# A layernorm, MLP and memory-attention kernel with its gradients: chains issued in a hand-written order, 512-wide output projections, left-over rows inside the forward chain

## Chip, cores and metric

The kernel runs on one core of one Trainium2 chip. The metric is the device time of one execution in microseconds. The engines are TensorE (PE, with its weight loads as PEld), VectorE (DVE), ScalarE (ACT), GpSimd (POOL) and SyncE (SP, which here issues the DMAs). SBUF is the on-chip memory, PSUM the memory that PE writes its results to.

## The reference

The output is the input plus two branches on its layernorm: an MLP with a squared ReLU, and an attention that runs over segments of 32 rows with 8 rows of memory. The kernel computes the output and the ten gradients of `jax.vjp`.

```python
xn = layernorm(x)                                   # (2048, 512)
out = x + A(xn, mem0, Wq, Wk, Wv, Wo) + (relu(xn @ w1 + b1) ** 2) @ w2 + b2

def A(x, mem, Wq, Wk, Wv, Wo):                      # 32 heads of 128
    for s in range(64):
        h = concat([mem, x[32 * s:32 * s + 32]])    # 8 + 32 = 40 rows
        q, k, v = h @ Wq, h @ Wk, h @ Wv
        p = softmax(where(mask, q @ k.T * 128 ** -0.5, -1e9))
        o = (p @ v) @ Wo                            # sum over heads
        mem, out_s = o[:8], o[8:]                   # 32 output rows
    return concat(outs)
```

The memory that a segment starts with is made by the segment before. So the 64 segments run one after the other, forward, and again backward for the gradients.

## The kernel before

**Rows.** A segment has 40 rows: 8 of memory, 32 of input. The kernel packs them so that 4 groups of heads (HG) times 32 rows fill the 128 partitions, with 8 heads (KH) side by side in each group. 32 of the 40 rows, the memory and the last 24 input rows, make the *chain*. The first 8 input rows of a segment, the *left-over rows*, do not enter the next memory as queries, so their projections can be done ahead and their attention later, for four segments at once: 16 blocks of 4 × 8 = 32 rows. Their keys and values still take part in the chain's attention.

**Stages, in order of time.** (1) Layernorm, the MLP and its gradients, weight transposes; the change doesn't touch these. (2) Left-row projections: 16 blocks, three tensors each (lines 558 to 571). (3) The forward chain: 64 segments (585 to 656). (4) The left-over loop: 16 blocks, forward and backward of the left-over rows (673 to 736). (5) The backward chain: 64 segments from last to first (807 to 925). (6) A tail, in which `slot_side` gathers the operands of the weight gradients from DRAM, and (7) the weight gradients (956 and 970), 16 groups of 160 matmuls.

**One forward segment.** `proj` (401) multiplies the transposed rows hT (512 × 32, in four pieces of 128) with the resident weights Wqkv: the four head groups go to four strips of 32 partitions. `flip` (181) transposes the result per head with PE, through a PSUM tile. `scores` (425, with the mask at 419), `softmax` (435 to 439), `norm` (445 to 450), `turn` (458) and `weigh` (469, scaled at 474) make the weighted values ON; these are flipped into OT, and `gather` multiplies OT with Wo (484). Heads come in three parts, PARTS = ((0, 3), (3, 3), (6, 2)), so projections are 384, 384 and 256 columns wide. `gather` here sums over all 32 heads in place:

```python
for k in ks:
    for g in range(HG):
        for c in range(DC):     # four strips: the four 128-column pieces of the output
            nc.tensor.matmul(R[32 * c:32 * c + 32, 0:P], lhsT=XT[:, k, g, :], rhs=W[:, g * KH + k, c * P:(c + 1) * P], ...)
```

That is 128 matmuls of 128 columns for 8 × 4 heads. R then holds the 32 output rows; ACT casts it (Rb, 623), PE transposes it (ps_m), and ACT copies the first 8 rows into the next hT (632), to which POOL has copied the 24 input rows. `rest`, played during the next segment, flips the values, and writes what the backward chain needs to DRAM: R as float32 (S_RF) and as bf16 (S_MBF), queries, keys and values (S_NA), probabilities (S_PA) and so on.

**One left-over block.** All DMA reads go into the pool `ls`, which has one buffer of each tile that is used late (l_N, l_kvM), and `ld`, which has two. `fetch_rows` (531, 532) reads the chain's rows and the left rows back from S_RF, to add them to the MLP branch and write the output.

**One backward segment.** The gradient rows goT are projected with WoT (401) and flipped (181), multiplied with the values (425), turned into gradients of the scores on DVE (494 to 500), and `outer` (508) makes the gradients of values, keys and queries: 192 matmuls of 16 to 40 columns. Three gathers (484) multiply these with the three transposed weights WT[2], WT[1], WT[0] into R (ps_gR). bRb (890), a transpose ps_bm and a copy (899) carry 8 rows to the segment before. `rest` flips all three gradients back (`spill_nat`, 24 transposes) and stores them to S_G. Every fourth segment also plays `left_done` (the left-over rows' gathers, ps_gRL, and their spill) and `finish_back` (layernorm's backward and the store).

**What sets the order.** The code is written segment by segment, and a scheduler orders the instructions of each engine by its own costs and priorities; the engines run their queues in order. All DMAs of these stages are issued by SP's queue. The tile pools decide which buffer a tile gets, and a tile whose buffer is still read waits.

Of the kernel before, what the change touches and what calls it, by code (L numbers as in the profile page):

```python
# [12 lines left out]
P = 128  # L13
# [13 lines left out]
def kernel(  # L27
# [80 lines left out]
    assert SEG == 32 and SPB == 4 and H == 32 and NL == 32 and 2 * KK == KH and KK * P == 512  # L108
    AROWS = NSEG * SEG
    NROW = AROWS + NB * NL  # L110
    RC_ALL = NROW // P

    PARTS = ((0, 3), (3, 3), (6, 2))
# [14 lines left out]
    S_TM = dram.tile([NB, P, 2, KH, HG, NL], BF16, name="S_TM")  # L128
    S_VTA = dram.tile([NSEG, P, KH, HG, L], BF16, name="S_VTA")
    S_PA = dram.tile([NSEG, P, KH, L], BF16, name="S_PA")  # L130
    S_PG = dram.tile([NB, P, 2, KH, 2 * NL], BF16, name="S_PG")
# [4 lines left out]
    S_RF = dram.tile([NSL, DC, SEG, P], F32, name="S_RF")  # L136
    S_RB = dram.tile([NSL, DC, SEG, P], F32, name="S_RB")
# [36 lines left out]
    zeros_bf = const.tile([M, D], BF16, name="zeros_bf")  # L174
    nc.vector.memset(zeros_bf[:], 0.0)
# [198 lines left out]

    def sb(name, bufs, side=None):
        return tc.tile_pool(name=name, bufs=bufs, side=side, reuse_waits="tile")
# [4 lines left out]
    def act_copy(out, in_):  # L381
        nc.scalar.copy(out, in_)  # L382

    def dve_copy(out, in_):
        nc.vector.tensor_copy(out, in_)  # L385
# [4 lines left out]
    def make_ops(big, trp, scp, wk, sm):  # L390
        def pbig(name):
            return big.tile([P, 512], F32, name=name, tag="big")

        def proj(dst, hT, W, col0, part, copy):

            k0, nk = part
            ps = pbig("ps_proj")
            for dc in range(DC):
                for g in range(HG):
                    c = col0 + g * GW + k0 * P  # L400
                    nc.tensor.matmul(ps[32 * g:32 * g + 32, 0:nk * P], lhsT=hT[:, dc, :], rhs=W[:, dc, c:c + nk * P],  # L401
                                     start=(dc == 0), stop=(dc == DC - 1), tile_position=(0, 32 * g))
            copy(dst[:, k0 * P:(k0 + nk) * P], ps[:, 0:nk * P])

        def flip(dst, srcN, part, copy):

            k0, nk = part
            ps = trp.tile([P, 1024], BF16, name="ps_tr", tag="tr")
            for k in range(nk):
                transpose_to(ps[:, k * P:(k + 1) * P], srcN[:, (k0 + k) * P:(k0 + k + 1) * P])  # L410
            copy(dst, ps[:, 0:nk * P].rearrange("p (k g r) -> p k g r", k=nk, g=HG))

        def scores(qT, kTs, part, mask):

            k0, nk = part
            sc = scp.tile([P, 512], F32, name="ps_sc", tag="sc")
            sc3 = sc[:, 0:nk * KW].rearrange("p (k n) -> p k n", k=nk)
            if mask is not None:
                nc.tensor.matmul(sc3, lhsT=ident[:], rhs=mask[:, 0:nk, :], start=True, stop=False,
                                 skip_group_check=True)  # L420
            for k in range(nk):
                c = 0
                for kT, n in kTs:
                    for g in range(HG):
                        nc.tensor.matmul(sc3[32 * g:32 * g + 32, k, c:c + n], lhsT=qT[:, k0 + k, g, :],
                                         rhs=kT[:, k0 + k, g, :], start=(mask is None), stop=True,
                                         tile_position=(0, 32 * g), skip_group_check=True)
                    c += n
# [581 lines left out]
```

## Time and profile before

| | us |
|---|---|
| median of 3 runs | 5021.1 |
| lowest and highest run | 5014.1, 5024.96 |
| the profiled execution | 5070.06 |
| its span, first to last instruction | 5068.2 |
| PE busy in the span | 3680.1 |
| weight loads (PEld) busy | 2250.3 |
| DVE, ACT, POOL busy | 1507.3, 1253.2, 313.2 |

The span has 89788 matmuls and 89874 weight loads, and a mean granted PE clock of 0.844. The profile's views give a line of the code for each group of instructions, the tile that it writes and, behind "<-", what it reads; numbers behind a name are buffers. "PEclk" is the share of the full clock that PE was granted. A row of a waits view says: engine, tile, line <- what ended the wait: us in total, times, longest. "issue" is time in which the engine waited for nothing that the profile shows. Windows count from the span's start.

### The profile page before, as it was taken

The page shows a single profiled execution, that of the slowest core. Times are in us where ns is not written, and L with a number is a line of the kernel's source. Part 1 is how long each engine was busy: PE and PEld are TensorE (multiplying, and loading weights), DVE is VectorE, ACT ScalarE, POOL GpSimd, SP SyncE. Part 2 cuts the span into 40 slices and gives each one's busy share as a digit, 9 for nine tenths or more (in the row PEclk, how much of TensorE's full clock was granted, in tenths as well). Part 3 has the DMA queues.
Part 4 walks back from the last instruction along what each step waited for, and adds up shares of the span by engine and source line. Part 5 has one row for each costly group of instructions (what it writes and reads, how often), then busy time and mean ns, then how long its engine had stood idle before and what let it go on. Part 6 is the DMA issues. An engine that isn't in the chain of part 4 may idle for free.

```text
span 5068.2 us, 195611 instructions
## 1 busy us (share of the span) xinstructions
PE 3680.1 (73%) x89788; PEld 2250.3 (44%) x89874; DVE 1507.3 (30%) x5110; ACT 1253.2 (25%) x3450; POOL 313.2 (6%) x741
## 2 busy tenths in 40 slices
PE   3950658878888888844446888787888788659999
PEld 1520223444444444422224666566666566524444
DVE  5530002333333333323333333333333333300000
ACT  1310014333333333311111222222222222201111
POOL 0000000111111111100000000000000000000000
PEclk8975989898888988866666888888888888879999
DMA  4377564233333233355443333333333333388886
GB/s 144 115 172 215 163 235 173 95 102 104 109 106 105 99 105 104 105 213 155 151 146 129 110 113 106 108 113 110 113 105 106 116 110 112 111 160 174 175 174 133
DMA packets 459571, 670.79 MB, mean 132 GB/s; under 512 B 172129, under 2 KB 285434, under 8 KB 456442
## 3 DMA queue, kind: packets, MB, share of 16 engines
q1 hardware_dynamic: 458746, 658.28, 43.9%
q8 instruction: 702, 11.50, 1.0%
q14 instruction: 123, 1.01, 0.1%
HBM read 347.75 MB, written 289.94 MB: 126 GB/s over the span
## 4 chain that ended last, share of the span: by engine, by line
PE 59%; DMA 14%; issue 8%; DVE 8%; ACT 8%; SPq 3%; POOL 0%; ACTq 0%; POOLq 0%; DVEq 0%
PE ps_proj L401 11%; PE ps_gR L484 11%; PE ps_gw L956 7%; PE ps_tr L181 5%; PE ps_R L484 4%; PE ps_nat L181 3%; PE ps_gkq L508 3%; PE ps_gwo L970 3%; DMA l_kvM<-S_NA 2%; PE ps_gRL L484 2%; PE ps_wgh L469 2%; DVE ON L474 2%; ACT OT L382 2%; DMA S_WT<-wtt 1%; DMA ghn<-S_GH1N 1%
## 5 line engine op out<-in xcount | busy, mean ns | idle before, releaser
L401 PE MATMUL ps_proj<-Wqkv,hT 128*32 128x384 bf16 x9216 | 569.0, 349 | 0.6 <-ACT hT L581 0.3
L956 PEld LDWEIGHTS <-HNc 128*128 128x128 bf16 x1920 | 187.5, 98 | 316.3 <-issue 93.9
L484 PE MATMUL ps_gR<-WT_39551,gk 128*32 128x128 bf16 x8192 | 238.9, 274 | 69.2 <-issue 55.3
L401 PEld LDWEIGHTS <-hT 128*32 128x32 bf16 x9216 | 223.1, 103 | 127.7 <-issue 36.9
L469 PEld LDWEIGHTS <-ET 32*32 32x32 bf16 (+1 forms) x5120 | 113.3, 104 | 315.1 <-issue 296.3
L382 ACT CAST gk<-ps_gkq 128x192 bf16<-128x192 f32 (+1 forms) x256 | 70.0, 274 | 717.5 <-PE ps_gkq L508 717.5
L484 PE MATMUL ps_gR<-WT_48383,gq 128*32 128x128 bf16 x8192 | 204.4, 265 | 33.4 <-issue 32.1
L484 PE MATMUL ps_gR<-WT_39549,gv 128*32 128x128 bf16 x8192 | 205.3, 255 | 29.0 <-issue 27.9
L385 DVE CAST gk<-ps_gkq 128x192 bf16<-128x192 f32 (+1 forms) x256 | 73.4, 287 | 512.8 <-PE ps_gkq L508 512.7
L484 PE MATMUL ps_R<-Wo,OT 128*32 128x128 bf16 x8192 | 170.7, 238 | 75.8 <-ACT OT L382 75.4
L484 PEld LDWEIGHTS <-gk 128*32 128x32 bf16 x8192 | 176.6, 122 | 101.6 <-issue 67.3
L401 PE MATMUL ps_proj<-WoT,goT 128*32 128x384 bf16 (+1 forms) x3072 | 207.0, 320 | 19.0 <-POOL goT L798 18.6
L474 DVE TENSOR_TENSOR ON<-ps_wgh,sm_rs 128x384 bf16<-128x384 f32 (+1 forms) x192 | 97.9, 510 | 404.5 <-PE ps_wgh L469 404.5
L484 PEld LDWEIGHTS <-gq 128*32 128x32 bf16 x8192 | 178.4, 123 | 45.7 <-issue 44.9
L385 DVE COPY gNat<-ps_nat 128x512 bf16<-128x512 bf16 x240 | 101.9, 424 | 308.9 <-PE ps_nat L181 308.9
L484 PEld LDWEIGHTS <-gv 128*32 128x32 bf16 x8192 | 164.0, 115 | 44.4 <-issue 37.5
L484 PEld LDWEIGHTS <-OT 128*32 128x32 bf16 x8192 | 133.0, 105 | 111.7 <-ACT OT L382 111.7
L469 PE MATMUL ps_wgh<-l_kvM,ET 32*32 32x128 bf16 x512 | 41.2, 299 | 192.3 <-DMA l_kvM<-S_NA 190.3
L382 ACT COPY gNat<-ps_nat 128x512 bf16<-128x512 bf16 x240 | 140.7, 586 | 144.0 <-PE ps_nat L181 140.9
L508 PEld LDWEIGHTS <-b_QK 32*128 32x128 bf16 x4096 | 123.3, 93 | 93.6 <-issue 68.0
L347 PE MATMUL ps_w_2827<-ghn,xnN 128*128 128x512 bf16 x16 | 6.5, 405 | 191.0 <-DMA ghn<-S_GH1N 191.0
L382 ACT COPY OT<-ps_tr 128x384 bf16<-128x384 bf16 (+1 forms) x192 | 85.2, 444 | 212.2 <-PE ps_tr L181 208.2
(952 smaller groups left out, 6957.4 us busy)
## 6 DMA issues: line engine op xcount, KB each, us to landing
S_G<-gNat SPq DMA_DIRECT2D x80, 768.0 KB
b_QK<-S_NA SPq DMA_DIRECT2D x64, 512.0 KB
S_VTA<-vT SPq DMA_DIRECT2D x64, 320.0 KB
b_vT<-S_VTA SPq DMA_DIRECT2D x64, 320.0 KB
S_O<-ON SPq DMA_DIRECT2D x64, 256.0 KB
ghn<-S_GH1N SPq DMA_DIRECT2D x32, 448.0 KB
an<-S_AN SPq DMA_DIRECT2D x32, 448.0 KB
S_WT<-wtt SPq DMA_DIRECT2D x48, 256.0 KB
```

The lines of the kernel that those rows point to most:

```text
L181: nc.tensor.transpose(ps_ap, in_ap, ident[base:base + k, base:base + k])
L347: nc.tensor.matmul(pss[k][:, :nf], lhsT=xnN[:, rc, dc * P:(dc + 1) * P], rhs=ghn[:, f0g:f0g + nf], start=(rc == 0), stop=(rc == TC - 1),)
L382: nc.scalar.copy(out, in_)
L385: nc.vector.tensor_copy(out, in_)
L401: nc.tensor.matmul(ps[32 * g:32 * g + 32, 0:nk * P], lhsT=hT[:, dc, :], rhs=W[:, dc, c:c + nk * P], start=(dc == 0), stop=(dc == DC - 1), ...
L469: nc.tensor.matmul(ps[32 * g:32 * g + 32, k * P:(k + 1) * P], lhsT=ET[32 * g:32 * g + n, k, i, :], rhs=V[32 * g:32 * g + n, (k0 + k) * P:( ...
L474: nc.vector.tensor_tensor(out=dst[:, k0 * P:(k0 + nk) * P].rearrange("p (k e) -> p k e", k=nk), in0=ps[:, 0:nk * P].rearrange("p (k e) -> ...
L484: nc.tensor.matmul(R[32 * c:32 * c + 32, 0:P], lhsT=XT[:, k, g, :], rhs=W[:, g * KH + k, c * P:(c + 1) * P], start=(first and k == ks[0] a ...
L508: nc.tensor.matmul(out(ps[g], k), lhsT=N_[32 * g:32 * g + m, k * P:(k + 1) * P], rhs=X(k)[32 * g:32 * g + m], start=first, stop=last, tile ...
L956: nc.tensor.matmul(ps[:], lhsT=HNc[:, rc, dc * P:(dc + 1) * P], rhs=gn[:, rc, u * 512:(u + 1) * 512], start=(rc == 0), stop=(rc == RC_ALL ...
L970: nc.tensor.matmul(ps[:], lhsT=on[:, rc, i * P:(i + 1) * P], rhs=GOc[:, rc, :], start=(rc == 0), stop=(rc == RC_ALL - 1))
```

## The change

**Order.** The forward chain, the left-over rows' backward and the backward chain run under `tc.manual_schedule()`: every instruction stands in the order in which Python plays it. Each step of a segment is a small function with a name (`k0mm` projects the first half of the keys, `k0fl` flips it, `k0Te` copies it out of PSUM, and so on), and one table for each chain lists the names in order: F_ORDER, LB_ORDER and B_ORDER. Slots in the tables (F0 to F2, X0 to X2, and others) take left-over work from F_FILL and B_FILL.

**Halves.** Heads go in two halves of 4, so every projection is 512 columns wide: 32 matmuls a tensor, where the three parts took 48.

**Gather.** `gather` now puts the four *head groups* into the four strips and streams all 512 output columns: 32 matmuls of 512 columns. The four strips then hold four partial sums, which are copied to SBUF as float32 (`ra` on ACT, `rv` on DVE, 256 columns each) and added by `sumup`, four matmuls with the float32 selection matrix `sel`. These leave the result transposed, as the next segment needs it, so Rb, ps_m and hT's copies go.

**On chip.** The transposed rows of all segments stay in SBUF: HT (forward) and GT (backward), each 512 × 2048, into whose segment slices the 8 memory rows are cast. S_MBF, S_MBB, S_RF and S_RB go. XT collects the rows of a block, and `block_rows` transposes them on PE.

**Left-over rows.** Their forward is played inside the forward chain, one block during the four segments behind it (the last block alone, after the chain). Their backward is a loop of its own, `lback`, with two buffers and a prefetch of one block. WT is loaded after its first block.

**PSUM.** `ring` makes one tile of one or two banks with two slots a bank for flips (f_tr, b_tr) and scores (f_sc, b_sc); the backward outer products use halves of one four-bank tile (b_pp). Most other tiles of the chains have one buffer.

**Tail.** `slot_side` loads S_HT and S_GM whole and transposes them on PE, 64 transposes each; GOc is made after the first group of products.

In PE's program, the end of a forward segment; before, OT is the operand of the gather, Rb the cast result, N the next tile to flip:

```order
L484 LDWEIGHTS OT
L484 MATMUL ps_R<-Wo,OT 32x128
L181 LDWEIGHTS Rb
L181 MATMUL ps_m<-ident,Rb 128x128
L181 LDWEIGHTS N_15540
L181 MATMUL ps_tr<-ident,N_15540 128x128
```

After, at the same place (f_N holds the segment's projections, f_sc is the ring of the scores):

```order
L457 LDWEIGHTS f_OT
L457 MATMUL ps_R<-Wo,f_OT 32x512
L464 MATMUL f_sc<-sel,R_7758 128x32 x4
L184 LDWEIGHTS f_N
L184 MATMUL f_tr<-ident,f_N 128x128
```

The cast and the transpose of R gave way to four matmuls of 32 columns, and the flip of the values that `rest` held now follows directly.

In DVE's program, the border between two backward segments, before:

```order
L385 CAST gk<-ps_gkq 128x2x32
L385 CAST gq<-ps_gkq 128x2x32
L385 CAST gkL<-ps_gkq 128x2x8
L901 COPY bRf<-ps_gR 128x128
L385 COPY gNat<-ps_nat 128x512 x6
L385 COPY gOT<-ps_tr 128x384 x2
L494 TENSOR_TENSOR ds_t<-ps_sc,b_P 128x120
L496 TENSOR_REDUCE ds_r<-ds_t 128x3
L498 TENSOR_TENSOR ds_u<-ps_sc,ds_r 128x120
```

After (R_50154 is the float32 copy of the gather, GT the gradient rows, gNat a gradient flipped back):

```order
L390 COPY R_50154<-ps_gR 128x256
L390 CAST GT<-b_sc 128x4x8
L390 COPY gNat<-b_tr 128x512 x2
L390 COPY b_XT<-b_sc 128x4x24
L390 COPY gNat<-b_tr 128x512 x2
L390 CAST gON<-ps_proj 128x512
L481 TENSOR_TENSOR ds_t<-b_sc,b_P 128x160
L485 TENSOR_REDUCE ds_r<-ds_t 128x4
L489 TENSOR_TENSOR ds_u<-b_sc,ds_r 128x160
```

DVE now carries the memory rows itself, between half of the copy of R and the copies of the flipped gradients, and one of the two casts of the projection.

In SP's program, the DMAs of one left-over block, before:

```order
L682 DMA l_kvM<-S_NA 32x1x2048 x4
L679 DMA l_TM<-S_TM 128x2048
L531 DMA l_acc<-S_RF 24x4x128 x4
L734 DMA bb<-S_B 128x512
L701 DMA S_O<-l_ON 128x1024
L704 DMA S_RF<-l_Rf 128x128
L685 DMA l_gT<-S_GT 128x4x128
L717 DMA S_GOL<-l_gON 128x1024
L532 DMA l_acc<-S_RF 8x4x128 x4
L677 DMA l_T<-S_TL 128x3072
L718 DMA S_PG<-l_PG 128x1024
L729 DMA S_GQL<-gqL 128x1024
```

After, one round of `lback`:

```order
L883 DMA l_gT<-S_GT 128x4x128
L884 DMA l_vTM<-S_VTM 128x1024
L885 DMA l_vTL<-S_TL 128x1024
L886 DMA l_P<-S_PL 128x512
L888 DMA l_kM<-S_NA 32x1x1024 x4
L889 DMA l_kL<-S_NL 128x1024
L931 DMA S_GOL<-l_gON 128x1024
L932 DMA S_GSL<-l_gS 128x512
L933 DMA S_GQL<-l_gq 128x1024
```

The reads of the next block now stand ahead of this round's stores, which are those of the block before; the output's reads and stores have moved into the forward chain.

The diff, cut to its core:

```diff
-    PARTS = ((0, 3), (3, 3), (6, 2))
-    S_MBF = dram.tile([NSEG, DC, SEG, P], BF16, name="S_MBF")
-    S_MBB = dram.tile([NSEG, DC, SEG, P], BF16, name="S_MBB")
+    S_HT = dram.tile([P, DC, S], BF16, name="S_HT")
+    S_GM = dram.tile([P, DC, S], BF16, name="S_GM")
...
+    sel = const.tile([P, SEG], F32, name="sel")
+    nc.vector.tensor_reduce(sel[:], identF[:].rearrange("p (g r) -> p r g", g=HG), axis=AX.X, op=ALU.add)
...
-        def gather(R, XT, W, ks, first, last):
-            for k in ks:
+    def gather(R, XT, W, h, first, last):
+        for k in range(4 * h, 4 * h + 4):
+            for g in range(HG):
+                nc.tensor.matmul(R[32 * g:32 * g + 32, :], lhsT=XT[:, k, g, :], rhs=W[:, g * KH + k, :],
+                                 start=(first and k == 4 * h), stop=(last and k == 4 * h + 3),
+                                 tile_position=(0, 32 * g))
+    def sumup(sc, R4):
+        for c in range(DC):
+            nc.tensor.matmul(sc[:, c * SEG:(c + 1) * SEG], lhsT=R4[:, c * P:(c + 1) * P], rhs=sel[:],
+                             start=True, stop=True)
+    def ring(pool, banks, width, dt, name):
+        t = pool.tile([P, 2 * banks, width], dt, name=name)
+        n = [0]
+        def take(_):
+            n[0] += 1
+            return t[:, n[0] % (2 * banks)]
+        return take
...
+    F_ORDER = (
+        "ld kl k0mm k1mm k0ev k1ev q0mm q0ev q1mm k0fl k1fl q1ev k0Te q0fl k1Te q0Te v0mm q1fl v0ev q1Te s0 s1 km "
...
+    with sb("fw", 1) as fw, psum("fbig", 4) as fbig, psum("fps", 1) as fps, ExitStack() as fstack:
+        HT = fw.tile([P, DC, S], BF16, name="HT")
+        dma(HT[:], S_XNT[:])
+        tr = ring(fps, 2, 4 * P, BF16, "f_tr")
+        scp = ring(fps, 2, 4 * KW, F32, "f_sc")
...
+            o["rv"] = lambda: vcp(st["R4"][:, 256:512], ps["R"][:, 256:512])
+            def HTf():
+                if s + 1 < NSEG:
+                    vcp(HT[:, :, (s + 1) * SEG:(s + 1) * SEG + M], crows(ps["S"])[:, :, 0:M])
...
+        with tc.manual_schedule():
+            for s in range(NSEG):
+                tables.append(fwd(s))
+                b, j = divmod(s, SPB)
+                if j == 0 and b > 0:
+                    lefts[b - 1] = left(b - 1)
+                play(F_ORDER, tables, s, F_LAG)
...
+            for b in range(NB + 1):
+                play(LB_ORDER, [x[0] for x in lb], b, LB_LAG)
+                if b == 0:
+                    for t in (2, 1, 0):
+                        dma(WT[t][:], S_WT[:, t, :, :])
...
+    with sb("bq", 1) as bq, sb("bs", 2) as bs, sb("bt", 1) as bt, psum("bpp", 1) as bpp, psum("bbig", 2) as bbig, \
+            psum("bps", 1) as bps:
+        GT = bq.tile([P, DC, S], BF16, name="GT")
+        pp = bpp.tile([P, 4, 512], F32, name="b_pp")
+        tr = ring(bps, 1, 4 * P, BF16, "b_tr")
+        scp = ring(bps, 1, 4 * KW, F32, "b_sc")
...
+            sT = p5.tile([P, DC, S], BF16, name="sT", tag="sT")
+            dma(sT[:], srcT[:])
+            for rc in range(TC):
+                ps = p5tr.tile([P, 4 * P], BF16, name="ps_side", tag="tr")
+                for dc in range(DC):
+                    transpose_to(ps[:, dc * P:(dc + 1) * P], sT[:, dc, rc * P:(rc + 1) * P])
```

More of the change, by code (lines that the diff above doesn't have):

```diff
@@ L534, with play @@
+    ENG = {"A": acp, "V": vcp}
+    def play(order, tables, s, lag):
+        for nm in order:
+            t = s - (1 if nm in lag else 0)
+            if 0 <= t < len(tables) and nm in tables[t]:
+                tables[t][nm]()
     wo_cm = sb("wo", 1, "right")
```

1092 lines of the change are left out of this document (626 added, 466 removed), and 10 rows, old and new, of tables (B_FILL, F_FILL).

## The prediction

> **What bounds the kernel now.** I read the slices of the page first, then the table of busy time by stage. Of the page, the granted clock in the 40 slices and the queue of instruction pages:
>
> ```profile
> PEclk8975989898888988866666888888888888879999
> q8 instruction: 702, 11.50, 1.0%
> ```
>
> The stages are left-row projections, forward chain, left-over loop, backward chain, tail, weight grads (columns: us; busy time of PE, PEld, DVE, ACT, POOL with instructions; PEclk; DMA share; GB/s):
>
> ```profile
> 705.00:882.00 177.00, 135.87 (x1928) 62.86 (x1932) 38.36 (x69) 69.96 (x124) 5.71 (x19) 0.91 0.57 208
> 882.00:2187.00 1305.00, 1055.23 (x25738) 590.47 (x25730) 489.66 (x1722) 466.99 (x1276) 181.90 (x505) 0.88 0.30 102
> 2187.00:2722.00 535.00, 215.52 (x7063) 138.67 (x7059) 169.34 (x425) 80.22 (x180) 43.28 (x68) 0.62 0.53 173
> 2722.00:4403.00 1681.00, 1359.77 (x50259) 1031.80 (x50260) 621.27 (x2566) 455.64 (x1593) 70.82 (x109) 0.85 0.34 107
> 4403.00:4486.00 83.00, 8.88 (x365) 7.24 (x366) 4.62 (x11) 3.24 (x7) 3.57 (x3) 0.59 0.86 181
> 4486.00:5068.00 582.00, 554.01 (x2508) 249.56 (x2557) 0.00 (x0) 75.02 (x128) 0.00 (x0) 1.00 0.78 164
> ```
>
> The two chains are 64 segments each: 1305/64 = 20.4 us and 1681/64 = 26.3 us a segment, with PE busy 81% of both. The left-over loop has PE busy 40% and 535/16 = 33 us a block. What ends PE's waits, in the left-over loop, in the forward chain, in the backward chain:
>
> ```profile
> PE ps_wgh L469 <- DMA l_kvM<-S_NA: 190.3, 60, 9.7
> PE ps_sc L425 <- DMA l_acc<-S_RF: 42.3, 1, 42.3
> ```
> ```profile
> PE ps_R L484 <- ACT OT L382: 75.2, 176, 0.6
> PE ps_tr L181 <- DVE ON L474: 75.2, 128, 0.7
> ```
> ```profile
> PE ps_gR L484 <- issue: 112.8, 132, 2.4
> PE ps_gkq L508 <- issue: 76.9, 59, 2.6
> PE ps_gRL L484 <- issue: 49.5, 33, 3.4
> ```
>
> So the left-over loop waits for one DMA chain, the forward chain for handoffs between PE, ACT and DVE, and the backward chain for "issue": 112.8 + 76.9 + 49.5 = 239 us in which nothing that the profile shows holds PE up, 3.7 us a segment. A stretch of the backward chain's critical pieces (start, us, what) shows their form:
>
> ```profile
> 3478.75 1.80 issue
> 3480.55 1.97 PE ps_gRL L484 x128
> 3482.52 2.05 issue
> ```
>
> 128 matmuls with their 128 weight loads run between two gaps. Queue q8 moved 11.50 MB in 702 packets, 16.4 KB each. I read the gaps as PE outrunning the arrival of its own program, 256 instructions at a time. The forward chain has no such wait: it issues (25738 + 25730)/1305 = 39 PE instructions a us, the backward chain 60, and 128 in the row above.
>
> The Trainium skill ("Runtime: NRT & Kernel Launch", section "Instruction fetch mechanics") has pages of 256 instructions too, but calls the crossing "mostly hidden"; here the trace disagrees by up to 239 us. By that page the gaps would be something else and could stay, the rival "gaps stay" below.
>
> A gap costs a second time. Two windows behind another gap (columns as above):
>
> ```profile
> 3587.00:3589.00 2.00, 0.05 (x4) 0.05 (x7) 0.00 (x0) 0.00 (x0) 0.00 (x0) 1.00 0.00 0
> 3589.00:3592.00 3.00, 3.00 (x111) 2.80 (x111) 0.00 (x0) 0.11 (x1) 0.00 (x0) 0.53 0.02 5
> ```
>
> After 2 us without work the clock is granted at 0.53 for 3 us. A mean clock c thus means a cold share of 2(1 − c): 24% forward (0.88), 30% backward (0.85).
>
> **Part by part**, against the profiled execution's 5070 us (span 5068.2), which is 49 us over the runs' median of 5021.1; I take 49 off at the end.
>
> *PE work of a segment.* Busy time by line, windows 905:2165 (1260/20.4 = 61.8 segments) and 2745:4382 (1637/26.3 = 62.3 segments); rows in the order line 401, 484, 181, 469 forward, then 401, 484, 181, 508 backward:
>
> ```profile
> 905.00:2165.00 1260.00, 548.29 (x8884) 214.49 (x8880) 0.88 0.30 103
> 905.00:2165.00 1260.00, 163.49 (x7856) 127.47 (x7856) 0.88 0.30 103
> 905.00:2165.00 1260.00, 242.53 (x2032) 123.93 (x2032) 0.88 0.30 103
> 905.00:2165.00 1260.00, 109.32 (x3928) 80.90 (x3928) 0.88 0.30 103
> 2745.00:4382.00 1637.00, 202.71 (x3017) 64.34 (x3017) 0.85 0.34 108
> 2745.00:4382.00 1637.00, 713.23 (x29568) 585.02 (x29568) 0.85 0.34 108
> 2745.00:4382.00 1637.00, 246.89 (x2412) 146.89 (x2412) 0.85 0.34 108
> 2745.00:4382.00 1637.00, 245.15 (x11904) 191.78 (x11904) 0.85 0.34 108
> ```
>
> What 512 columns cost stands in the left-row projections of before, and beside it a 384-column run under a low clock:
>
> ```profile
> 857.04 2.56 PE L401 MATMUL ps_proj<-Wqkv,hTL 128*32 128x512 bf16 x44
> 1507.72 1.51 PE L401 MATMUL ps_proj<-Wqkv,hT 128*32 128x384 bf16 x16
> ```
>
> 58 ns a matmul warm, so 16 of them (a half of one tensor, or half a gather) take 0.93 us; cold, 94 ns for three quarters of the columns. The backward gathers are 713.23/62.3 = 11.4 us a segment, the left rows' among them. After: 6 × 16 matmuls = 5.6 us, plus the left rows' 5.6 us once per four segments = 1.4. The projections go from 3.25 to 1.9. PE rows fall from 179,750 to 110,187.
>
> *The sum over head groups* (four float32 matmuls against sel) has no row in before. Below stand four bf16 128x128 transposes, 0.44 us (242.53 × 4 / 2032 = 0.48 at this clock); above, four times that, 1.9. I take 1.0, nearer the lower, since only 32 columns stream. Copies around it, and the other steps of the chain:
>
> ```profile
> L388 ACT COPY dTL<-ps_tr 128x512 bf16<-128x512 bf16 x61 | 35.8, 587 | 45.7 <-DMA S_TL<-dTL 23.5 <-PE ps_tr L181 19.8 <-DVE dNL L388 1.2
> L388 DVE CAST dNL<-ps_proj 128x512 bf16<-128x512 f32 x34 | 23.5, 691 | 116.5 <-DMA S_NL<-dNL 106.3 <-PE ps_proj L401 9.0 <-ACT dNL L388 1.2
> L388 DVE COPY dTL<-ps_tr 128x512 bf16<-128x512 bf16 x35 | 14.9, 425 | 40.3 <-DMA S_TL<-dTL 18.3 <-PE ps_tr L181 16.7 <-PE ps_proj L401 3.9
> L437 DVE TENSOR_TENSOR sm_t<-ps_sc,sm_mx 128x120 f32<-128x120 f32 x186 | 50.0, 269 | 10.0
> L858 ACT CAST gv<-ps_gv 128x256 bf16<-128x256 f32 x248 | 80.1, 375 | 39.5 <-PE ps_gv L508 38.4
> ```
>
> *Forward, a warm segment walked in the written order:* k and q projections 4 × 0.93 = 3.7; then one ring tile for all flips, so that engines take turns: flip 0.4, ACT 0.59, flip 0.4, DVE 0.43, ACT 0.59, flip 0.4, DVE 0.43 = 3.2 (v's projection runs under it); second half of the scores, mostly hidden by the first, 0.8; maximum, subtraction, sum and transpose on DVE with the exponentials on ACT 2.0 (about 7 steps near 0.27 us); two weighings 109.32/61.8 = 1.8 and a flip of v 0.4; scaling 0.69 and flip 0.4; two half gathers 1.9; copies of R on ACT and then DVE 0.8, sum 1.0, cast into HT with its handoffs 0.3. Sum 17.0; I add 0.4 for left-row work that doesn't fit into PE's gaps: 17.4. Of it 11.0 is PE time (3.7 + 1.2 + 0.8 + 2.2 + 0.4 + 1.9 + 1.0, less 0.2 of overlap), which doubles when cold; at before's 24% that is 2.6: 20.0 a segment, 1280 us, and about 15 for the last block's left rows, played alone: −10. So the shorter work is given back to whole-tile handoffs. Ends: 17.4 a segment (−180) and 22 (+115).
>
> *Backward:* projections 1.9, transposes 246.89/62.3 = 4.0, scores 0.75 (as forward), outer products 245.15/62.3 = 3.9, gathers 5.6, sum 1.0: 17.1 us; waits of PE 1.2 at the tail (copies of R and the cast into GT, with nothing else to run) and about 1.0 at the head (projection to ACT to flip to ACT to scores, partly under the other half): 19.3. Left rows 1.4 gathers + 0.2 sum and transposes = 1.6. Instructions: about 925 in 22 us, 42 a us, near forward's 39, which shows no gaps; so I let the 239 us go. The 224 waits on which they fell, with 3 us of low clock behind each long one, could make up most of the cold 30% (504 us); I take 12%, on the 14 us of PE time that I count on the path (18.7 less what runs under waits): 1.7. 19.3 + 1.6 + 1.7 = 22.6, 1446 us: −235. Ends: 20 (−400) and 24.6 (−105).
>
> *Left-over stage.* Its forward half goes into the forward chain; the rest is one pipelined pass. The old chain at its start, one block's wait, and the rate of a large load:
>
> ```profile
> 2208.61 25.98 DMA l_TM<-S_TM
> ...
> 2259.03 8.80 DMA l_kvM<-S_NA
> ```
> ```profile
> 694.00 33.38 DMA Wqkv<-in_A_Wv_dram
> ```
>
> 12.6 MB in 33.4 us is 377 GB/s. New: WoT (4.2 MB, 11 us), two blocks' loads, and WT (12.6 MB, 33 us), which SP queues ahead of block 2's: about 60 us until block 2 can run. A block moves 1.3 MB in and 0.6 out, 9 us at the page's usual 210 GB/s and about 6 by its DVE and PE work; I take 8.8. 60 + 14 × 8.8 + 13 to load GT and start = 196, with the last block's drain 205: −330 (−355 to −250).
>
> *The rest.* HT (2 MB, 6 us) loads behind Wqkv and is copied before the first projection: +8 (0 to +30). The tail loses the float32 left rows' round trip and the scattered loads, but the last read stays:
>
> ```profile
> 4441.83 10.40 DMA GOc<-in_grad_out_dram
> ...
> 4463.35 22.00 DMA gn_107955<-S_G
> ```
>
> 83 becomes 55: −28. GOc's 64 transposes behind the first product group: 8 us, +8.
>
> Sum: +8 − 10 − 330 − 235 − 28 + 8 = −587; 5070 − 587 = 4483, less 49: 4434, **4435 us**.
>
> **Rivals.** *Warm chains:* if shorter waits keep the clock up and left rows fit in gaps, 17.4 and 20.0 (19.3 with 0.7 for left rows) a segment: another 64 × (2.6 + 2.6) = 333 less, 4100. For it: the projections' 0.91 in the first row. Against: forward has no issue waits and is still at 0.88.
>
> *Gaps stay:* page crossings stall at 42 instructions a us too, or the gaps have another cause: 4435 + 239 = 4675. Against it: forward at 39 shows none.
>
> *Whole-tile handoffs cost more* (a sum near 1.9, waits on one-bank rings, left-row work queued ahead of the chain on PE): forward 22, backward 25: 64 × (2.0 + 2.4) = +282, 4715.
>
> *Slower:* the clock stays low in both chains. The other terms, the last block's 15 us among them, bring −327, so the two segments together must grow by 5.1 us to lose, from 46.7 to 51.8. Warm they are 37.4, all cold 37.4 + 11 + 14 = 62.4; it decides from a cold share of 58%, a clock of 0.71. At the left-over loop's 0.62, 76% cold, they are 56.4, 9.7 more: 64 × 9.7 − 327 = +294, 5021 + 294 = 5315. Against it: the waits that I count are under 1.5 us each, shorter than the 2 us gap above.
>
> The Trainium skill ("TensorE: Matmul & The Clock Gate", Part 1) lets the clock fall only after an idle window of about 3.4 us; the 0.53 after 2 us here shows a shorter idle stretch to be enough. By that page chains whose waits are all shorter would run warm, the first rival.
>
> **How the numbers follow.** Forecast 0.56, its own range 4300 to 4560; warm 0.18, gaps stay 0.10, handoffs 0.11, slower 0.04, and 0.01 that gains and losses meet. The range 4140 to 4720 leaves out the slower case and the lower edge of the warm one. A measurement can tell about 0.2%, 10 us, from no change: faster 0.95, same 0.01, slower 0.04.
>
> **What would show it.** Right: the waits by "issue" are nearly gone in the backward chain; chain stages of 1280 and 1446 us; a left-row pass near 200 us; sums of about 1 us each. Wrong: a chain stage beyond its ends, a clock under 0.8 in the chains, or a left-row pass over 285 us, each of which would say which term was mis-sized.

## The result, and the profile after

The changed kernel takes 4416.4 us, the median of four runs (4411.7 to 4429.8). The kernel before took 5023.0 beside it. The ratio is 0.880, 95% interval 0.878 to 0.882. The profiled execution took 4414.6 us, with a span of 4412.7.

The granted clock in the 40 slices and the queue of instruction pages, after:

```profile
PEclk8995797989999999998558989898899898799999
q8 instruction: 441, 7.23, 0.7%
```

Busy time by stage, after, in the columns of the prediction (left-row projections, forward chain, what lies between the chains, backward chain, tail, weight gradients):

```profile
719.00:870.00 151.00, 134.88 (x1924) 54.75 (x1924) 65.50 (x97) 57.68 (x99) 0.00 (x0) 0.98 0.45 167
870.00:2073.00 1203.00, 983.55 (x19754) 545.50 (x19755) 567.62 (x1489) 449.69 (x1017) 169.75 (x413) 0.94 0.34 120
2073.00:2312.00 239.00, 104.40 (x2870) 59.83 (x2869) 84.27 (x192) 46.09 (x88) 6.39 (x20) 0.56 0.69 238
2312.00:3755.00 1443.00, 1116.79 (x27048) 618.34 (x27048) 566.61 (x1535) 410.80 (x872) 33.77 (x30) 0.90 0.34 115
3755.00:3812.60 57.60, 21.26 (x225) 15.14 (x222) 12.03 (x26) 7.82 (x16) 3.47 (x3) 0.63 0.85 224
3812.60:4412.70 600.10, 566.61 (x2624) 254.80 (x2624) 3.57 (x8) 79.31 (x136) 0.00 (x0) 0.98 0.77 163
```

The chains fell from 1305 to 1203 us and from 1681 to 1443, and the stage between them from 535 to 239. The backward chain issues (27048 + 27048)/1443 = 37 PE instructions a us, where it was 60, and the granted clock is up in both chains. What ends PE's waits now, first in the forward chain, then in the backward chain (us in total, times, longest):

```profile
PE f_tr L184 <- ACT f_kT L387: 46.3, 64, 1.0
PE f_tr L184 <- ACT f_vT L387: 39.4, 64, 1.2
PE f_tr L184 <- DVE f_N L390: 37.6, 29, 3.4
```
```profile
PE b_tr L184 <- DVE gNat L390: 75.7, 63, 3.6
PE b_tr L184 <- ACT gNat L387: 71.9, 90, 2.8
PE ps_gR L457 <- ACT gk L387: 47.8, 64, 0.7
```

No row of PE's waits in the backward chain says "issue" any more. Its place is taken by copies out of PSUM, gNat ahead of all: the gradients that are flipped back and stored to S_G.

### The profile page after: what moved, and what is told of

The parts are those of the page before. It is cut to its first block, busy times and chain, and to the rows that moved or that the text cites. A ratio compares the mean times of both kernels' runs of the same rounds, so it can differ in the third digit from the quotient of the medians.

```text
span 4412.7 us, 125551 instructions
## 1 busy us (share of the span) xinstructions
PE 3279.5 (74%) x56408; PEld 1717.3 (39%) x56408; DVE 1484.0 (34%) x3666; ACT 1153.9 (26%) x2371; POOL 220.8 (5%) x501
## 5 line engine op out<-in xcount | busy, mean ns | idle before, releaser
L403 PE MATMUL ps_proj<-Wqkv,HT 128*32 128x512 bf16 x6144 | 385.3, 394 | 4.0 <-DVE HT L628 0.3
L184 PE MATMUL f_tr<-ident,f_N 128*128 128x128 bf16 x1536 | 145.9, 227 | 95.1 <-ACT f_kT L387 46.3
L403 PEld LDWEIGHTS <-HT 128*32 128x32 bf16 x6144 | 149.8, 98 | 157.9 <-issue 18.0
L457 PE MATMUL ps_gR<-WT_31348,gk 128*32 128x512 bf16 x2048 | 140.4, 396 | 71.5 <-ACT gk L387 47.8
L387 ACT CAST f_N<-ps_proj 128x512 bf16<-128x512 f32 x256 | 146.0, 582 | 131.8 <-DMA S_NA<-f_N 69.4
L387 ACT COPY gNat<-b_tr 128x512 bf16<-128x512 bf16 x240 | 139.8, 590 | 135.5 <-PE b_tr L184 86.9
L403 PE MATMUL ps_proj<-WoT,GT 128*32 128x512 bf16 x2048 | 155.8, 458 | 10.0 <-POOL GT L964 10.0
L457 PE MATMUL ps_gR<-WT_31347,gv 128*32 128x512 bf16 x2048 | 162.2, 473 | 0.1
L457 PE MATMUL ps_R<-Wo,f_OT 128*32 128x512 bf16 x2048 | 141.6, 425 | 0.0
L457 PE MATMUL ps_gR<-WT_31349,gq 128*32 128x512 bf16 x2048 | 139.8, 395 | 0.0
```

The lines of the kernel that those rows point to most:

```text
L184: nc.tensor.transpose(ps_ap, in_ap, ident[base:base + k, base:base + k])
L403: nc.tensor.matmul(ps[32 * g:32 * g + 32, :], lhsT=hT[:, dc, :], rhs=W[:, dc, c:c + 4 * P], start=(dc == 0), stop=(dc == DC - 1), tile_pos ...
L457: nc.tensor.matmul(R[32 * g:32 * g + 32, :], lhsT=XT[:, k, g, :], rhs=W[:, g * KH + k, :], start=(first and k == 4 * h), stop=(last and k ...
```

## The experiments

All were timed beside the kernel before on the same chip. Spans of a chain are from the first to the last start of its projections, "between" is what lies between them. Small differences of spans say little: the backward chain takes 1428 to 1452 us in the six kernels that have it as changed, and the kernel before takes 5023 to 5056 us on the chips used.

| kernel | median us | ratio to before | forward | between | backward |
|---|---|---|---|---|---|
| before | 5023.0 | 1 | 1305 | 536 | 1660 |
| changed | 4416.4 | 0.880 (0.878 to 0.882) | 1193 | 249 | 1428 |
| narrow_gather | 4824.1 | 0.955 (0.952 to 0.958) | 1251 | 247 | 1769 |
| before_wide | 5006.2 | 0.990 (0.987 to 0.993) | 1508 | 587 | 1365 |
| split_rings | 4351.1 | 0.861 (0.859 to 0.863) | 1119 | 248 | 1435 |
| half_stores | 4377.2 | 0.866 (0.863 to 0.868) | 1196 | 250 | 1398 |
| early_store | 4400.3 | 0.873 (0.870 to 0.875) | 1145 | 249 | 1452 |
| spread_weights | 4426.5 | 0.876 (0.874 to 0.878) | 1197 | 247 | 1436 |
| no_left_forward | 4516.9 | 0.894 (0.892 to 0.896) | 1301 | 233 | 1437 |
| no_left_early | 4512.5 | 0.893 (0.887 to 0.900) | 1284 | 232 | 1434 |
| scheduler_order | 4239.6 | 0.840 (0.838 to 0.841) | 1235 | 209 | 1255 |
| mixed_whole | 4101.6 | 0.812 (0.811 to 0.814) | 1078 | 221 | 1257 |
| mixed_halves | 3991.7 | 0.790 (0.788 to 0.792) | 1082 | 221 | 1153 |
| scheduler_rings | 3932.3 | 0.779 (0.777 to 0.780) | 1029 | 208 | 1155 |

### narrow_gather: were the issue waits a matter of PE's instruction count?

```diff
-                nc.tensor.matmul(R[32 * g:32 * g + 32, :], lhsT=XT[:, k, g, :], rhs=W[:, g * KH + k, :], ...)
+            for c in range(DC):
+                for g in range(HG):
+                    nc.tensor.matmul(R[32 * g:32 * g + 32, c * P:(c + 1) * P], lhsT=XT[:, k, g, :],
+                                     rhs=W[:, g * KH + k, c * P:(c + 1) * P], ...)
```

> The changed kernel with only its gathers cut back into pieces of 128 columns (four matmuls of 128 columns in place of one of 512; strips by head group, sum and order as in the changed kernel). PE's program grows from 110,187 to 171,627 rows; a backward segment from about 925 to 1,600 rows. Theory A, that PE's unexplained waits were its program arriving too slowly: the waits by 'issue' come back in the backward chain, 150 us or more in total, each near 2 us, and the backward chain grows from 1445 us by the narrow matmuls' own time (24 against 14.5 ns for each 128 columns, 4 us a segment, 270 us) and by these waits, to 1850 us or more; the forward chain, at about 800 rows a segment and 39 rows a us, grows by under 80 us and shows no such waits. Total 4800 to 5000 us. Theory B, that the waits belonged to something else in the old program (the scheduler's order, or the strips): 'issue' stays under 30 us, the total is near 4750 us.

PE's waits in its backward chain:

```profile
PE ps_gR L458 <- issue: 99.6, 111, 2.9
...
PE ps_gRL L458 <- issue: 49.0, 37, 2.6
...
PE b_pp L538 <- issue: 26.2, 22, 2.9
```

The unexplained waits are back, 175 us in these three rows, in the hand order, with the new strips and the sum; only the gathers' matmuls have changed, four times as many and a quarter as wide. The total is in theory A's range. The backward chain's span grew by 341 us, but its stage takes 1790 us, less than theory A's 1850, and the waits last 1.0 us on average (2.9 at most), not 2. The forward chain, at 43 rows a us, grew by 58 us and has 26 us of such waits, where none were expected. This version computes a wrong gradient of mem0 and is read for its times alone.

The traces say more about these waits. Counted along PE's matmuls and weight loads, the issue waits over 0.5 us stand a multiple of 256 instructions apart, to within 2: all 180 in the backward chain of the kernel before, all 134 in this one's, and all 22 in this one's forward chain. And each of them ends 1.0 to 1.6 us after a packet of q8, the queue of instruction pages, has landed, while moments picked at random in the same chains lie anywhere from 0 to 4 us and more behind such a packet. So PE does wait for the next page of its program.

### before_wide: the wide gather alone

```diff
+        def sumup(R):
+            R4 = wk.tile([P, D], F32, name="R4", tag="R4", bufs=1)
+            nc.scalar.copy(R4[:, 0:256], R[:, 0:256])
+            nc.vector.tensor_copy(R4[:, 256:512], R[:, 256:512])
+            R2 = pbig("ps_sum")
+            for c in range(DC):
+                nc.tensor.matmul(R2[32 * c:32 * c + 32, 0:P], lhsT=sel[:], rhs=R4[:, c * P:(c + 1) * P],
+                                 start=True, stop=True, tile_position=(0, 32 * c))
```

> The kernel before, with one part of the change alone: gathers of 512 columns with strips by head group, the copies of R as float32 and the sum with sel (here with sel as the weights, so that the result lies as R lay before and all that follows is unchanged). The scheduler, the thirds, the left-over loop and the DRAM copies stay. PE's program falls from 179,750 to 118,518 rows. Theory A (program arrival): the issue waits of the backward chain fall from 239 to under 40 us, and it shrinks from 1681 us by these, by 5 us of gather a segment and by part of the cold clock, less 2 us a segment for copies and sum: 1250 to 1420 us. The forward chain gets longer by 0.5 to 1.5 us a segment, 30 to 100 us. Total 4650 to 4850 us. Theory B (the waits belong to the old order): issue stays above 150 us and the total is 4900 us or more.

Its two chains, by the columns of the stage table:

```profile
870.00:2390.00 1520.00, 1247.46 (x20242) 574.37 (x20235) 520.69 (x1794) 493.61 (x1347) 182.32 (x507) 0.73 0.26 90
...
2968.00:4352.00 1384.00, 1279.39 (x28115) 688.08 (x28116) 649.42 (x2646) 483.48 (x1673) 70.54 (x109) 0.99 0.40 129
```

The backward chain did what theory A said: issue waits of 3 us in place of 239, a clock of 0.99, and 295 us off the span, more than the changed kernel's 232. So the backward gain belongs to the wide gather; the rest of the change, the hand order included, adds nothing to it there. The forward chain missed: 203 us longer, where 30 to 100 were expected. The stage between the chains grew by 51 us, and the total is 5006 us where theory A had at most 4850. In the forward chain PE's idle time is nearly the same, 273 us against 250, but PE is busy for longer, 1247 us against 1055, because the clock is at 0.73: busy time times clock is 911 us, against 929 before. Most of its segments take 23.9 us, over 3 us more than before. The total gain is 1%. I had priced the longer serial tail by its length alone, and not that the clock could come down behind it; that the tail is what brought it down is argued here, not tested.

### scheduler_order: the hand order alone

```diff
-        with tc.manual_schedule():
+        with ExitStack():
```

(three times: forward chain, left-over backward, backward chain)

> The changed kernel with the three hand orders given to the scheduler of the kernel before (the tables are still played, so the program is written in the same sequence, but the scheduler may move instructions); all else as changed. Theory A, that the hand order earns the forward chain's gain and nothing in the backward chain: the forward chain goes from 1203 us to 1280 or more, the backward chain stays within 60 us of 1445. Theory B, that the sequence in which the tiles are reused sets the time whoever orders it: both chains within 30 us of the changed kernel's.

Both theories fell. The forward chain is 42 us longer, so the hand order is worth something there, less than theory A's 77. But the backward chain is 174 us shorter, and the stage between 40 shorter. PE's waits for gNat in the backward chain go from 148 to 62 us, those for gk from 72 to under 40, with the same tiles: the scheduler has moved other PE work into them. Where the hand order flips a piece of gv and then one of gk, with a wait of 0.67 us between, the scheduler's trace has a gather between the two.

### split_rings: whole-tile handoffs

```diff
+        if banks == 2:
+            ts = [pool.tile([P, width], dt, name="%s%d" % (name, i)) for i in range(2)]
+            def take(_):
+                n[0] += 1
+                return ts[n[0] % 2]
+            return take
```

> The changed kernel with the forward chain's two PSUM rings (flips, scores) as two separate tiles each, one per bank, in place of one tile with four slots. In the changed kernel PE waits 46 + 39 + 11 = 97 us in the forward chain for ACT's copies out of the flip ring (f_kT, f_vT, f_qT). Theory A, that these are waits for the whole ring tile and not for the slot: they fall to under 40 us, and the forward chain shrinks from 1203 us by 40 to 90 us. Theory B, that the copies themselves are the chain: the forward chain stays within 20 us.

PE's waits in its forward chain:

```profile
PE f_tr L184 <- ACT f_vT L387: 47.5, 64, 1.4
...
PE f_tr L184 <- ACT f_kT L387: 31.8, 64, 0.8
```

Theory A holds for the time, 74 us off the span, with two slots in place of four. It doesn't hold for the waits: f_qT's is gone and f_kT's is shorter, but f_vT's stays, and 79 us are left where under 40 were expected. PE's waits for sm_t at the ring of the scores, 25.5 us in the changed kernel, are gone too. In all PE is idle for 44 us less, 175 against 219; the rest of the gain is less busy time, at a clock of 0.96 in place of 0.94. A segment went from 17.5 to 16.2 or 16.6 us.

### half_stores: the buffers of S_G's stores

```diff
-                        if n not in tl:
-                            tl[n] = bs.tile([P, GW], BF16, name="gNat", tag="gNat")
-                        f(tl[n][:, HC[p]], ps[n, p][:])
+                        h_ = bs.tile([P, 4 * P], BF16, name="gNat", tag="gNat", bufs=4)
+                        f(h_[:], ps[n, p][:])
```

> The changed kernel with the flipped-back gradients in four half-size buffers, each stored as soon as it is full, in place of two whole ones stored when both halves are in. In the changed kernel PE waits 76 + 72 = 148 us in the backward chain for the copies gNat, and these wait for the store of an earlier gNat to land (81 us on DVE alone). Theory A, that the stores' landing holds the two buffers: the waits fall below 80 us and the backward chain shrinks from 1445 us by 40 to 130 us. Theory B, that the copies' own time on DVE and ACT through a one-bank ring sets this: the backward chain stays within 20 us.

PE's waits in its backward chain:

```profile
PE b_tr L184 <- ACT gNat L387: 64.3, 93, 1.2
...
PE b_tr L184 <- DVE gNat L390: 42.1, 63, 0.8
```

The long waits are gone (1.2 us at most, where 3.6 was the longest), but 106 of 148 us stay and the span falls by 30 us, below theory A's 40 and above theory B's 20, so neither holds. In the hand order the stores' landing was the smaller part of this wait.

### early_store: the store of f_N

```diff
-                      "N": (fo, [P, 3, GW]), ...
+                      "N0": (fo, [P, GW]), "N1": (fo, [P, GW]), "N2": (fo, [P, GW]), ...
+            def sk():
+                for t in (1, 0):
+                    dma(S_NA[s].rearrange("g r t c -> (g r) t c")[:, t, :], T["N%d" % t][:])
```

(`sk` stands behind `q1Te` in F_ORDER)

> The changed kernel with the one buffer f_N of a segment's projections split into three, for queries, keys and values, and the stores of keys and queries queued right behind the last flip of the queries, half a segment earlier. In the changed kernel the first segment of most blocks takes 20 to 23 us, others 17.5; in one of them ACT waits 5.3 us for the store of f_N, DVE 4.6, PE 2.6, and the clock is 0.85. Theory A, that this wait makes those segments slow: they fall to 18.5 us or less, and the forward chain shrinks from 1203 us by 40 to 75 us. Theory B, that the block's loads and stores on SP's queue delay them anyway: within 20 us.

In the changed kernel most blocks' first segments take 20 to 23 us, the others 17.4 to 17.7. Here the first ones mostly take 17.8 to 19.5, and the span falls by 49 us: theory A for the span, though 11 of these 15 segments stay above its 18.5 us and a third of the excess is left. The backward chain, which the edit doesn't touch, took 24 us longer, so the total is only 16 us below the changed kernel's; why is open.

### no_left_forward and no_left_early: what left-over work in the chain costs

```diff
-            return o
+            return {n: (f if n in ("lo", "lb", "out") else (lambda: None)) for n, f in o.items()}
```

> The changed kernel without the left-over rows' forward in the forward chain: their scores, softmax, weighing, flips, gathers and sums are left out, and zeros are stored for their probabilities and values, so that the rows of the output and the gradients that depend on them are not computed. In the changed kernel the first four segments, which have no left-over work beside them, take 20 to 21.5 us at a granted clock of 0.74 to 0.81, later ones with that work mostly 17.5 at 1.00. Theory A, that the left-over work fills gaps in which PE's clock would fall: without it all segments run like the first four, 20 to 21 us, and the chain takes 1260 to 1340 us, longer than the 1203 us of the changed kernel with less to do. Theory B, that the first segments are slow for another reason (loads at the start) and left-over work costs what it takes: 17.2 us or less a segment, the chain at 1050 to 1130 us plus the store waits of every fourth segment.

> no_left_forward and early_store together: no left-over forward in the chain (the rows of the output and the gradients that depend on it are not computed) and three buffers with earlier stores. In no_left_forward all 63 segments took 19.6 to 21.5 us at a clock of 0.79 with no wait for f_N's store in the trace; in early_store the first three segments, with the same work and no left-over work beside it, took 17.2 to 17.4 at 1.00, behind the same waits of PE. Theory A, that the left-over work is what holds the clock up and early_store's first segments only started well: most segments at 20 us or more, span of the chain's projections above 1240 us. Theory B, that the same waits leave the clock up or bring it down by where they fall in time, which a shift of the stores changes: most segments at 17.2 to 17.5, span near 1090 us.

Four windows: a segment of the changed kernel without left-over work, its second; the same segment in early_store; then the whole forward chain of no_left_forward and of no_left_early:

```profile
889.60:910.30 20.70, 16.55 (x270) 8.27 (x268) 7.76 (x21) 6.34 (x14) 2.40 (x6) 0.77 0.23 84
```
```profile
896.00:913.30 17.30, 13.09 (x269) 7.13 (x267) 7.72 (x20) 6.37 (x14) 2.40 (x6) 1.00 0.28 100
```
```profile
872.00:2175.00 1303.00, 1036.48 (x16932) 538.04 (x16936) 491.68 (x1273) 405.22 (x893) 172.32 (x411) 0.79 0.29 101
```
```profile
872.00:2180.00 1308.00, 1028.28 (x17043) 536.75 (x17039) 495.06 (x1282) 408.90 (x899) 174.56 (x416) 0.80 0.30 104
```

Without the left-over work the chain has 14% fewer matmuls and takes 107 us longer. So that work is not just hidden: it fills waits in which the clock would otherwise come down, which is theory A in both runs. It isn't the whole of it. The first two windows hold the same work and the same waits of PE (1.5, 1.2 and 0.7 us the longest), and one runs at 0.77, the other at 1.00; no_left_early, too, has a few segments of 17.2 us between those of 20 and 21.

### spread_weights

```diff
-                if b == 0:
-                    for t in (2, 1, 0):
-                        dma(WT[t][:], S_WT[:, t, :, :])
+                if b in (0, 4, 8):
+                    t = 2 - b // 4
+                    dma(WT[t][:], S_WT[:, t, :, :])
```

> The changed kernel with the three loads of WT (4.2 MB each) queued behind blocks 0, 4 and 8 of the left-over backward loop in place of all three behind block 0. In the changed kernel PE waits 27 us there for the next block's l_goT, queued behind WT. Theory A, that these 27 us are only WT's transfer in the way: the stage between the chains, 225 us, shrinks by 12 to 30 us. Theory B, that the stage is bound by what moves in all (238 GB/s over it), or the backward chain then waits for WT: within 8 us.

Theory B: 247 us against 249 between the chains. PE's wait for l_goT falls from 27 to 20 us, but two later blocks, behind the loads that were moved, take 18 us in place of 10: a load costs its time wherever it is queued.

### The versions put together

mixed_halves: the hand order in the forward chain with split_rings' and early_store's tiles, the scheduler for the rest with half_stores' buffers. mixed_whole: the same with whole gNat buffers. scheduler_rings: mixed_halves with the scheduler in the forward chain as well.

> A version put together from the runs so far: the forward chain in the hand order with split_rings' tiles and early_store's three buffers; the left-over backward loop and the backward chain left to the scheduler, as in scheduler_order, with half_stores' buffers. Theory A, that the gains are of different waits and add up: forward chain 1050 to 1100 us (split_rings and early_store took 74 and 49 us off its span), backward chain 1230 to 1280 us, total 4030 to 4110 us on a chip where the kernel before takes 5050. Theory B, that they draw on the same waits or on the clock: the forward chain stays above 1120 us and the total above 4140.

> As mixed_halves, with the whole gNat buffers and stores of the changed kernel in the backward chain. Theory A, that the stores' landing still holds the buffers when the scheduler orders the chain (PE waited 62 us for gNat in scheduler_order): 15 to 50 us longer than mixed_halves. Theory B, that the scheduler has moved other work into these waits: within 10 us of mixed_halves.

> As mixed_halves, with the forward chain too left to the scheduler. Theory A, that the hand order is worth something in the forward chain, and nowhere else: its forward chain takes 1150 to 1220 us, 60 us or more longer than mixed_halves. Theory B, that scheduler_order's longer forward chain came from the shared ring tiles and the late store, which tie a scheduler more than a hand order: both within 30 us.

The chains and what lies between them in scheduler_rings:

```profile
870.00:1909.00 1039.00, 971.17 (x19799) 539.16 (x19800) 555.92 (x1492) 460.00 (x1019) 177.75 (x413) 0.99 0.42 142
1909.00:2109.00 200.00, 101.56 (x2863) 55.89 (x2862) 85.55 (x192) 48.76 (x89) 6.31 (x19) 0.66 0.79 270
2109.00:3285.00 1176.00, 1056.42 (x27160) 593.96 (x27164) 579.50 (x1543) 409.07 (x873) 34.80 (x31) 0.99 0.47 143
```

This version is the fastest, 3932.3 us, 0.779 of the kernel before and 0.885 of the changed kernel (0.7785/0.8799; the two medians, from different chips, give 0.890). PE is busy for 93% and 90% of the chains, at a clock of 0.99. mixed_halves went past its theory A: its forward chain, 1082 us, is in the range, but the backward chain, 1153, and the total are 77 and 38 us below what it expected. mixed_whole takes 110 us longer than mixed_halves, over twice theory A's 50. So half buffers are worth 104 us in the backward chain under the scheduler, 30 in the hand order; as I read it, a scheduler uses a buffer that a fixed order has nothing to put beside. Theory A of scheduler_rings fell: with split tiles and the earlier store the scheduler's forward chain is not 60 us longer than the hand order's but 53 shorter, past theory B's 30 as well. The hand order's small lead in scheduler_order came from the shared tiles and the late store together.

## Why the prediction was right, and where its terms were off

**The sum.** Forecast 4435, measured 4416. On the profile's own scale it was 4483 against 4414.6, 68 us too long; the 49 us taken off for the distance between profile and median have no counterpart after, where the profiled run lies 2 us under the median. So part of the closeness is luck. By stage, with the forecast in brackets: left-row projections −12 us (+8), forward chain −102 (−25), between the chains −296 (−315, the last block's 15 us included), backward chain −238 (−235), tail −25 (−28), weight gradients +18 (+8); in all −655 (−587).

**The issue waits** went as argued: gone from 239 us to no row, and narrow_gather brings them back with the instruction count, each a multiple of 256 instructions from the next and behind an instruction page that has just come. The rival that the gaps stay fell. The Trainium skill ("Runtime: NRT & Kernel Launch", section "Instruction fetch mechanics") calls the crossing of a page "mostly hidden": at 56 to 60 PE instructions a us the traces here disagree, at 37 to 43 they agree, but for the 26 us in narrow_gather's forward chain.

**Forward chain.** The warm walk gave 17.4 us with the left-over work, and segments without a disturbance measure 17.4 to 17.7. The step that was off is the cold share, taken over from before as 24%: it is 12% (clock 0.94), because left-over work fills the waits, as no_left_forward showed. The walk did not have the store of f_N, whose buffer the next segment's first copies need. ACT's waits for it, all 14 in a block's first segment:

```profile
ACT f_N L387 <- DMA S_NA<-f_N: 69.4, 14, 6.1
```

Together 1203 us in place of 1280. The sum of the head groups was priced well; one of them (each float32 matmul is recorded twice), in the timeline:

```profile
1421.86 1.09 PE L464 MATMUL f_sc<-sel,R_17256 128*128 128x32 f32 x8 [0.48 <-ACT R_17256 L387]
```

**Backward chain.** 1446 us forecast, 1443 measured, by two errors that happen to cancel. PE is busy 1116.8/64 = 17.4 us a segment, against 20.4 in the forecast (17.1, 1.6 and 1.7); it waits 5.1 us, against 2.2. More than half of the work's excess is the outer products (line 536, the backward window of after):

```profile
2312.00:3755.00 1443.00, 139.07 (x12288) 109.82 (x12288) 0.90 0.34 115
```

They take 139.07/64 = 2.2 us a segment, forecast at 3.9 as before: the same number of matmuls, but over four row strips in turn where before they went over two. The clock is not the reason: before_wide, with the old strips, takes 249 us for them at 0.99. That the strips are is argued, not tested alone. The other lines add up to 16.4 us, against 16.5 with the cold share in the forecast, and 1.1 us of work overlaps that the walk had laid end to end. The waits were underpriced by gNat's 2.3 us a segment, of which the walk had nothing. The clock came to 0.90, 20% cold, not 12%.

**Between the chains.** About 22 us of the 239 are the last block's forward, 15 in the forecast, with a wait of 7.3 us for its load; the rest is 217, against 205. PE's waits:

```profile
PE l_tr L184 <- ACT l_gON L387: 30.6, 14, 2.7
PE ps_proj L403 <- POOL l_goT L897: 27.4, 1, 27.4
...
PE ps_proj L403 <- DMA WoT<-S_WOT: 20.5, 1, 20.5
```

The loads of WoT and WT are there as worked out: block 2 starts 61 us into the loop, forecast at 60. The blocks behind it were mis-sized, at 10.1 us each and not 8.8. spread_weights shows that moving WT back doesn't help. In scheduler_order, 40 us shorter in this stage, a block takes about 8.1 us, so its handoffs were the part to shorten.

**The rest.** The left-row projections ended 12 us earlier, not 8 later. The first of them did start later, at 719 us and not 706, behind the load of HT; but from there on PE waits for 2 us in all, where before it waited 40, for the pieces of Wqkv and for the copies dNL and dTL. The sum had nothing of this. The tail is 57.6 us, forecast 55, and 13 of them are a wait before the first product, the first row below. The weight gradients grew by 18 us, not 8: GOc's transposes behind the first group take 8 us, as forecast, and PE then waits for the next operand, the second row:

```profile
PE ps_gw L1270 <- issue: 13.0, 1, 13.0
...
PE ps_gw L1270 <- DMA gn_67184<-S_G: 6.1, 1, 6.1
```

**The rivals.** Warm chains came true in scheduler_rings, with 1029 and 1155 us, below even the rival's 17.4 and 20.0 a segment. Whole-tile handoffs were real too, and separate tiles are worth 74 us, but they were in the walk already.

## What to carry to other kernels

When PE waits for nothing that the profile shows, count its instructions in a us against a stage without such waits, and see whether the waits stand a fixed number of instructions apart: here fewer, wider matmuls were the cure, and the order they stand in was not. A hand-written order pays for each tile that has one buffer, so first split the tiles and move the stores, then compare with the scheduler, which here won both chains. And when a chain's granted clock is under 1, price work that fills its waits at nothing or less, and suspect a longer tail of costing more than its own length.

## What was not expected of the hardware

Segments under a low clock settle into fixed periods. In no_left_forward they repeat every six segments, 20.6 + 20.0 + 21.5 + 21.2 + 19.6 + 20.0 = 122.9 us, and in before_wide most take 23.9 us. These are 36 and 7 times 3.41 us. The Trainium skill ("TensorE: Matmul & The Clock Gate", Part 1) describes a free-running window of 3413 ns by which the clock is set. The traces agree: the granted clock has two values, 0.5 and 1.0, and all its stretches, 198 in the changed kernel and 3200 in the fourteen traces, begin on a grid of 3.413 us. Some steps of that grid, from the changed kernel's first two segments (PE busy is the second number, the clock the third from the end):

```profile
878.51:881.92 3.41, 2.00 (x76) 1.38 (x72) 3.00 (x11) 1.82 (x5) 0.73 (x2) 1.00 0.22 84
881.92:885.34 3.42, 2.28 (x24) 1.11 (x28) 0.82 (x2) 1.07 (x2) 0.51 (x2) 0.50 0.65 248
...
888.75:892.16 3.41, 3.41 (x32) 1.87 (x36) 0.90 (x3) 0.24 (x1) 0.75 (x2) 0.50 0.24 82
892.16:895.58 3.42, 3.04 (x56) 1.45 (x49) 1.10 (x2) 1.47 (x3) 0.00 (x0) 1.00 0.28 86
```

Behind a step with PE busy for 2.00 of 3.41 us the clock falls, behind a full one it rises. In the whole changed kernel PE was busy for 0 to 76% of the step before each of the 98 falls, and for 76 to 100% before each of the 99 rises. No single wait as long as the step is needed: the longest of PE is 1.9 us in no_left_forward's segments and 1.0 in before_wide's. Two things stay open. The clock also stayed up behind steps with PE busy for as little as 44%, so no one share decides. And that the same waits cost nothing in one place and 3 us in another by where they fall on the grid is argued from this; no run here varied it alone.
